# Linformer attention and a gated feed-forward in one kernel: an earlier V projection in the first batch, reciprocals spread over slots in the second, and a split last output tile

## The chip, the core and the metric

The kernel runs on one core of a Trainium2 chip. The metric is the device time of one execution in microseconds (us); lower is better. Seven executions of the kernel before took 569.02 to 571.19 us, with a median of 570.72 us. One more was recorded by the hardware profiler; its times are the ones that the text works with.

The engines are called as the profile calls them: PE is TensorE (matmuls; PEld are its weight loads), DVE is VectorE, ACT is ScalarE, POOL is GpSimd and SP is SyncE, which here only issues DMAs.

## The reference

Two stages follow each other. B = 8 batches, H = 8 heads, S = 1024 positions, head width 64, 64 projected keys, model width 512, feed-forward width 1536:

```python
k_proj = einsum('ks,bhsd->bhkd', E, k)
v_proj = einsum('ks,bhsd->bhkd', F, v)
scores = matmul(q, k_proj.T) / sqrt(64)
attn = exp(scores - max) / (sum(exp(scores - max)) + 1e-09)
x = (attn @ v_proj)          # heads side by side: 8192 tokens x 512
gate = sigmoid(x @ w_gate)
out = (gate * (x @ w_val)) @ w_out
```

The kernel computes in bf16 with fp32 sums. It leaves out the maximum, since the scores are small, and writes the sigmoid as (tanh(x/2) + 1)/2; the halves are taken up by a factor 0.5 when an output tile leaves PSUM.

## The kernel before, in words

**Work.** Each batch has two blocks of 512 tokens. For a block the feed-forward runs 12 steps (`mstep`, m = 0 to 11): 4 matmuls of 128x128 by 512 columns for the gate into one PSUM bank, 4 for the value into another, then `gate`: ACT takes the tanh of the gate's bank (L224, `sig`), and DVE multiplies it into the value's bank and writes `hT` (L930). Afterwards `oproj` multiplies `hT` with `w_out`: 12 matmuls for each of four tiles of 128 tokens, DVE moves the tile from PSUM to `ost` (L957), and SP writes it out (L965). The feed-forward uses four PSUM banks (F0 to F3) in turn: a bank that an `mstep` fills must have been emptied by the `mstep` two before.

**Attention** for the next batch lies between these steps. In the program the main loop makes a list `todo` of slots (an `mstep` or an `oproj` each), and `put(i, fn)` places a piece of attention behind slot i; `spots` lists those places. Every engine takes its instructions strictly in the order in which the program adds them, and a semaphore wait holds up all that is behind it on that engine. The pieces are: the projection of k and v (`project`), the turning of k (`turn_k`), scores and their exponentials (`sc`, ACT writes `eT`), the spread sums (`den`: matmuls that leave the sum of exponentials of each query in PSUM, then reciprocals on DVE into `rden`), `split` (DVE writes the reciprocal as two bf16 parts into `rhl`), `bc` (matmuls spread `rhl` over 64 partitions, ACT copies the result to `rb`) and `xo` (attention times V, DVE multiplies with `rb` and writes `xT`, the input of the feed-forward).

**The first batch** has no feed-forward to lie beside. Its first half is computed at the very start, in an order written out by hand (L975 to L1006): k projected in two halves of four heads (`project`, `keep_k`, `turn_k`), q turned on PE (`qt(0)`, `qt(1)`), `sc(0)`, `den(0)`, `sc(1)`, V's first half (`v_part(0)`), `den(1)`, `bc(0)`, `xo(0)`, `bc(1)`, V's second half (`v_part(1)`), and then `xo(1)`, which is called from inside the first feed-forward step (`first_pair`, L898), behind its first two matmuls. `first_pair` first multiplies with the input rows that `xo(0)` wrote and then with those of `xo(1)`. `busy(n)` puts n matmuls of the identity into an otherwise unused bank. The banks for this stage come from a list, `whole` (L202). All loads go through POOL in the order k, q, v, then the weights in chunks (`start_loads`); each is a DMA on one queue.

**The second batch's attention** (`attention(1)`) lies in the second block of the first batch: slot 11 is the steps m = 0 and 1 of that block (`first_pair`), slots 12 to 21 are m = 2 to 11, and 22 to 25 are the four `oproj` of the first block. Its `den` (L761 to L780) is one piece: eight matmuls, then four reciprocals of 128x128 (L776), then behind the same slot 18 `split` (L785, L787); `bc(0)` is behind slot 21.

**The end.** After the last step the four output tiles of the last block are done one behind the other (L1082); nothing else is left then. SP waits for the last four writes (L1085).

Of the kernel before, what the change touches and what calls it, by code (L numbers as in the profile page):

```python
# [7 lines left out]
ALU = mybir.AluOpType  # L8
# [4 lines left out]
P = 128  # L13
# [105 lines left out]
def bass_linformer_attn__then__ffn_glu_sigmoid_kernel(  # L119
# [18 lines left out]
    with contextlib.ExitStack() as es:  # L138
# [52 lines left out]
        class Ring:  # L191
# [8 lines left out]
        A0, A1, A2, A3 = AB  # L200
        F0, F1, F2, F3 = FB
        whole = Ring(  # L202
            (A0, A1, A2, A3, F0, F1)
            + (A0, A1, F2, A2)
            + (A3, F0, F1)
            + (A0, A1, A3, F0)
            + (A2, F2, A0, A1, F1)
            + (A2, A3, A0, A1, A2, A3)
        )
        ffn, att = Ring(FB), Ring(AB)  # L210

        def mm(b, o, lhsT, rhs, r, start=True, stop=True, tp=None, tr=False):
            kw = {}
            if tp is not None:
                kw["tile_position"] = tp
            if tr:
                kw["is_transpose"] = True
            else:
                kw["start"], kw["stop"] = start, stop
            return add("PE", lambda e: e.matmul(o, lhsT, rhs, **kw), r=r, x=[("bank", b)])  # L220
# [5 lines left out]
        def dve(fn, r, w, b=None):  # L226
            x = [] if b is None else [("bank", b)]
            return add("DVE", fn, r=r, w=w, x=x)
# [218 lines left out]
        def busy(n):  # L447
            for _ in range(n):
                mm(FB[3], bank[FB[3]][:, 0:P], ident[:, :], ident[:, :], ["ident"])
# [47 lines left out]
        def turn_k(ring, R=None):  # L497
            bk = ring.next()
            ob = bank[bk][:, :].bitcast(BF16)
            rs = range(NR)[pairs(R)]  # L500
            for n, r in enumerate(rs):
                for g in range(2):
                    mm(
                        bk,
                        ob[64 * g : 64 * g + 64, n * P : (n + 1) * P],
                        kp[:, r, :],
                        ident[:, :],
                        [("kp", r // 2), "ident"],
                        tr=True,
                        tp=(0, 64 * g),  # L510
                    )
            act(
                kpD[:, 2 * rs[0] : 2 * rs[-1] + 2, :].rearrange("p h c -> p (h c)"),
                ob[:, 0 : P * len(rs)],
                [],
                [("kpD", x) for x in both(R)],
                b=bk,
            )
# [152 lines left out]

        def attention(b):
            s = b % 2

            def kv():
                bk = att.next()
# [81 lines left out]
            def den():  # L758
                bk = att.next()
                for rnd in range(2):  # L760
                    for j in range(4):  # L761
                        n = 4 * rnd + j
                        mm(
                            bk,
                            bank[bk][32 * j : 32 * j + 32, :],
                            dsel[:, n % 2, rnd, :],
                            eT[:, n, :],
                            [("dsel", n % 2), ("eT", n)],
                            start=(rnd == 0),
                            stop=(rnd == 1),  # L770
                            tp=(0, 32 * j),
                        )
                for c in range(4):
                    cc = slice(c * P, (c + 1) * P)
                    dve(
                        lambda e, cc=cc: e.reciprocal(rden[:, cc], bank[bk][:, cc]),  # L776
                        [],
                        [("rden", c, R) for R in range(2)],
                        b=bk,
                    )  # L780

            def split():
                rd = [("rden", c, R) for c in range(4) for R in range(2)]
# [74 lines left out]
            if b == 1:  # L858
                return [
                    k_alone,  # L860
                    lambda: turn_k(att),
                    v_alone,
                    lambda: sc(0),
                    lambda: sc(1),
                    den,
                    split,
                    lambda: bc(0),
                    lambda: bc(1),
                    lambda: xo(0),
                    lambda: xo(1),  # L870
                ]
# [68 lines left out]
                b=pv,  # L940
            )

        def oproj(blk, tt, pb):
            T = 4 * blk + tt
            for m in range(NF):
                mm(
                    pb,
                    bank[pb][:, :],
                    hT[blk % 2][:, m, tt * P : (tt + 1) * P],
                    wO[:, m, :],  # L950
                    [("hT", blk % 2, m), "wO"],
                    start=(m == 0),
                    stop=(m == NF - 1),
                )
            o = ost[T % 4]
            dve(
                lambda e: e.tensor_scalar(o[:, :], bank[pb][:, :], 0.5, None, op0=ALU.mult),  # L957
                [],
                [("ost", T % 4)],
                b=pb,  # L960
            )
            t = 2 * (2 * (blk % 2) + tt % 2) + tt // 2
            add(
                "SP",
                lambda e: e.dma_start(out_v[blk // 2, t], o[:, :]),  # L965
                r=[("ost", T % 4)],
                dma=f"out{T % 4}",
            )


        start_loads()
# [1 line left out]
        project_consts()  # L973
        busy(6)
        qt, sc, den, bc, xo = half_unit(0, whole)  # L975
        for R in range(2):
            bk = whole.next()
            project(0, 0, [bk, bk], 0, R)
            busy(3)
            keep_k(bk, 0, R)  # L980
            turn_k(whole, R)
            if R == 0:
                busy(6)

        def v_part(R, engines):
            bks = [whole.next(), whole.next()]
            project(1, 1, bks, 0, R)
            keep_v(bks, 0, engines, R)

        qt(0, ("DVE", "ACT"))  # L990
        busy(3)
        sc(0)
        qt(1, ("DVE", "DVE"))
        busy(6)
        den(0)
        sc(1)
        busy(4)
        v_part(0, ["ACT"] * 4)
        den(1)
        bc(0)  # L1000
        busy(4)
        xo(0)
        busy(4)
        bc(1)
        busy(6)
        v_part(1, ["ACT", "DVE", "ACT", "DVE"])  # L1006
        load_q(1)
        load_k(1)
        load_v(1)
# [16 lines left out]
        for b in range(B):  # L1026
            todo = []
            for blk in (2 * b, 2 * b + 1):
                ms = [[m] for m in range(NF)]
                if blk <= 1:  # L1030
                    ms = [[0, 1]] + ms[2:]
                if blk == 1:
                    gaps = {11: [0, 1, 2, 3]}
                else:
                    gaps = {2: [0], 5: [1], 8: [2], 11: [3]}
                for m in ms:
                    if len(m) == 2:
                        todo.append(
                            lambda blk=blk: first_pair(blk, None if blk else lambda: xo(1))
                        )  # L1040
                    else:
                        todo.append(lambda blk=blk, m=m[0]: mstep(blk, m))
                    if blk >= 1:
                        for tt in gaps.get(m[-1], ()):
                            todo.append(lambda blk=blk, tt=tt: oproj(blk - 1, tt, ffn.next()))
            at = {}

            def put(i, fn):
                at.setdefault(i, []).append(fn)

            if b == 0:
                qt2, sc2, den2, bc2, xo2 = half_unit(1, att)
                put(4, lambda: (qt2(0, ("DVE", "ACT")), qt2(1, ("DVE", "ACT"))))
                put(5, lambda: (sc2(0), sc2(1)))
                put(6, den2)
                put(8, lambda: (bc2(0), bc2(1)))
                put(9, lambda: (xo2(0), xo2(1)))
                spots = (12, 13, 15, 16, 17, 18, 18, 21, 22, 23, 24)
            else:
                spots = (3, 6, 10, 13, 16, 16, 20, 23, 26, 29)  # L1060
            if b + 1 < B:
                for i, fn in zip(spots, attention(b + 1)):
                    put(i, fn)
            def load_next(n):
                load_k(n)
                load_q(n)
                load_v(n)

            if b == 0:
                put(16, lambda: load_next(2))  # L1070
                put(24, lambda: transpose_q(2))
            else:
                if b + 2 < B:
                    put(4, lambda b=b: load_next(b + 2))
                    put(20, lambda b=b: transpose_q(b + 2))
            for i, slot in enumerate(todo):
                slot()
                for fn in at.get(i, ()):
                    fn()
            assert max(at, default=0) < len(todo)  # L1080
        last = 2 * B - 1
        for tt in range(4):  # L1082
            oproj(last, tt, ffn.next())

        plan.emit(nc, es, final=[f"out{i}" for i in range(4)])  # L1085


# [26 lines left out]
```

The softmax here doesn't subtract the row's maximum and nothing guards it: scores larger than these inputs give would overflow.

## Time and profile before

| what | value |
|---|---|
| median of seven executions | 570.72 us (569.02 to 571.19) |
| the profiled execution's own time | 571.03 us |
| its span, first to last instruction | 569.2 us |
| PE busy | 551.6 us, 97% of the span |
| DVE, ACT, POOL busy | 249.3, 177.0, 107.2 us |
| feed-forward matmuls, gate / value / out | 747 / 752 / 750 records of 379 ns each, one every 0.2155 us where nothing waits |
| L776, the four reciprocals of 128x128 | 28 in seven batches, 909 ns each |
| L957, one output tile out of PSUM | 64, 692 ns each |

The time lies 1.83 us above the span; that part is outside of the program's instructions. A matmul record is longer than its share of the engine, since matmuls are pipelined: the distance from one start to the next is what counts. "Idle before <- releaser" in a row says how long the engine had nothing to do ahead of the instruction, and which engine's work (or DMA) let it go on. Idle time costs only where it lies on the chain that sets the end.

### The profile page before, as it was taken

What the parts mean: (1) busy time and instruction counts of PE and PEld (TensorE: products, weight loads), DVE (VectorE), ACT (ScalarE), POOL (GpSimd) and SP (SyncE); (2) the same over time, 40 slices, a digit from 0 to 9 for tenths busy, and PEclk for the clock granted to TensorE, in tenths of its full rate; (3) what the DMA queues carried; (4) which work ended last, traced back from release to release, by engine and by line L of the source; (5) the groups of instructions that cost most, each with busy time, mean ns of one, the idle gap of its engine ahead of it and who ended that gap; (6) DMA issues with size and microseconds to landing.
All of it is one profiled execution on the core that took longest, in us unless ns stands there. A gap on an engine that the chain in (4) does not pass through costs nothing.

```text
span 569.2 us, 7617 instructions
## 1 busy us (share of the span) xinstructions
PE 551.6 (97%) x2958; PEld 246.5 (43%) x3013; DVE 249.3 (44%) x398; ACT 177.0 (31%) x312; POOL 107.2 (19%) x148
## 2 busy tenths in 40 slices
PE   5999989999999999999999999999999999999997
PEld 4544434444444444444444444444444444444443
DVE  3644364344633546325443256335363354533332
ACT  2554631432133322352223422243213332222220
POOL 9400201007200090002600054000700007000000
PEclk9999999999999999999999999999999999999999
DMA  9999899935845059512677046560601001010012
GB/s 164 198 201 187 140 212 172 204 86 115 136 88 102 21 113 183 90 50 59 116 143 121 23 105 110 118 102 37 114 18 48 37 22 39 37 38 30 26 37 92
DMA packets 76420, 56.00 MB, mean 98 GB/s; under 512 B 34688, under 2 KB 67968, under 8 KB 76384
## 3 DMA queue, kind: packets, MB, share of 16 engines
q0 software_dynamic: 33984, 29.89, 34.7%
q1 hardware_dynamic: 42400, 25.63, 17.6%
q8 instruction: 23, 0.38, 0.3%
q14 instruction: 13, 0.11, 0.1%
HBM read 60.29 MB, written 16.78 MB: 135 GB/s over the span
## 4 chain that ended last, share of the span: by engine, by line
PE 94%; DVE 2%; DMA 1%; issue 1%; ACT 1%; POOL 0%; DVEq 0%; POOLq 0%
PE pF L220 87%; PE pA L220 7%; DMA KV<-in_k_dram 1%; ACT eT L224 1%; DVE rden L776 1%; DVE hT L930 0%; DVE xT L645 0%; ACT sig L224 0%; DVE rden L593 0%; DVE ost L957 0%; DVE vpD L495 0%; DVE rhi L785 0%; POOL quad L313 0%; DVE rhl L596 0%; DVE rhi L594 0%
## 5 line engine op out<-in xcount | busy, mean ns | idle before, releaser
L930 DVE SCALAR_TENSOR_TENSOR hT<-sig,pF 128x512 bf16<-128x512 f32 x192 | 130.7, 685 | 201.0 <-PE pF L220 146.8
L224 ACT ACTIVATE sig<-pF 128x512 f32<-128x512 f32 x192 | 114.4, 599 | 319.0 <-PE pF L220 315.4
L220 PE MATMUL pF<-xT,wV 128*128 128x512 bf16 x752 | 195.9, 379 | 2.7 <-DVE hT L930 1.9
L220 PE MATMUL pF<-xT,wG 128*128 128x512 bf16 x747 | 194.5, 379 | 2.5 <-issue 1.5
L220 PE MATMUL pF<-wO,hT 128*128 128x512 bf16 x750 | 173.9, 379 | 1.5 <-issue 0.8
L220 PEld LDWEIGHTS pF<-xT,wV 128*128 128x128 bf16 x768 | 74.9, 98 | 93.0 <-DVE hT L930 2.9
L220 PEld LDWEIGHTS pF<-wO,hT 128*128 128x128 bf16 x768 | 73.9, 98 | 93.0 <-issue 6.2
L220 PEld LDWEIGHTS pF<-xT,wG 128*128 128x128 bf16 x768 | 72.1, 98 | 95.0 <-issue 12.2
L822 POOL PARTITION_BROADCAST rb<-rrow x96 | 70.8, 798 | 217.1 <-DMA rrow<-rden 212.0
L957 DVE TENSOR_SCALAR ost<-pF 128x512 f32<-128x512 f32 x64 | 44.3, 692 | 103.7 <-PE pF L220 103.7
L224 ACT ACTIVATE eT<-pA 128x512 bf16<-128x512 f32 x63 | 32.7, 606 | 8.7 <-PE pA L220 8.7
L847 DVE TENSOR_TENSOR xT<-pA,rb 128x512 bf16<-128x512 f32 x56 | 34.7, 682 | 0.0
L776 DVE RECIPROCAL rden<-pA 128x128 f32<-128x128 f32 x28 | 23.7, 909 | 0.0
L238 POOL DMA_DIRECT2D KV<-in_v_dram x9 | 7.8, 874 | 84.4 <-PE pF L220 84.4
L220 PE MATMUL pA<-KV,EFT 128*64 128x512 bf16 (+2 forms) x168 | 16.0, 332 | 0.6 <-DMA KV<-in_k_dram 0.6
L224 ACT ACTIVATE kpd<-pA 64x1024 bf16<-64x1024 f32 x6 | 6.1, 1017 | 28.3 <-PE pA L220 28.3
L238 POOL DMA_DIRECT2D KV<-in_k_dram x9 | 8.0, 889 | 32.1 <-PE pF L220 32.1
L220 PEld LDWEIGHTS pA<-KV,EFT 128*64 128x64 bf16 x168 | 8.3, 115 | 8.1 <-issue 3.4
L220 PE MATMUL pA<-eT,vpD 64*64 64x512 bf16 (+1 forms) x140 | 10.4, 366 | 0.3 <-DVE vpD L495 0.3
L220 PE MATMUL pA<-qT,kpD 64*64 64x512 bf16 (+1 forms) x140 | 10.7, 370 | 0.0
L224 ACT ACTIVATE vpD<-pA 64x512 bf16<-64x512 f32 (+2 forms) x20 | 9.7, 485 | 1.6 <-PE pA L220 1.2
L238 POOL DMA_DIRECT2D Qb<-in_q_dram x11 | 9.4, 865 | 0.0
(70 smaller groups left out, 91.4 us busy)
## 6 DMA issues: line engine op xcount, KB each, us to landing
out_dram<-ost SPq DMA_DIRECT2D x64, 256.0 KB, 2.1
Qb<-in_q_dram POOLq DMA_DIRECT2D x7, 1024.0 KB, 15.3
KV<-in_k_dram POOLq DMA_DIRECT2D x7, 1024.0 KB, 11.2
KV<-in_v_dram POOLq DMA_DIRECT2D x7, 1024.0 KB, 11.7
wO<-in_moe_w_out_dram POOLq DMA_DIRECT2D x1, 1536.0 KB, 12.0
wG<-in_moe_w_gate_dram POOLq DMA_DIRECT2D x5, 256.0 KB, 18.4
wV<-in_moe_w_val_dram POOLq DMA_DIRECT2D x5, 256.0 KB, 19.0
KV<-in_k_dram POOLq DMA_DIRECT2D x2, 512.0 KB, 8.9
```

Source lines behind the costliest of these rows:

```text
L220: return add("PE", lambda e: e.matmul(o, lhsT, rhs, **kw), r=r, x=[("bank", b)])
L224: return add("ACT", lambda e: e.activation(o, i, func, scale=scale), r=r, w=w, x=x)
L238: add("POOL", lambda e: e.dma_start(o, i), r=r, w=w, dma=sem)
L776: lambda e, cc=cc: e.reciprocal(rden[:, cc], bank[bk][:, cc]),
L822: lambda e, n=n, i=2 * rnd + c, j=j, parts=parts: e.partition_broadcast(rb[0:parts, n, :], rrow[32 * j : 32 * j + 1, i, :], channels=parts),
L847: lambda e, r=r, g=g, n=n, bk=bks[g]: e.tensor_tensor(xT[s][:, r, :, 256 * g : 256 * g + 256], bank[bk][:, :].rearrange("p (f c) -> p f c" ...
L930: lambda e: e.scalar_tensor_tensor(hT[blk % 2][:, m, :], sg[:, :], 1.0, bank[pv][:, :], ALU.add, ALU.mult,),
L957: lambda e: e.tensor_scalar(o[:, :], bank[pb][:, :], 0.5, None, op0=ALU.mult),
```

## The change

There are three edits. The first is in the first batch: `qt(0)` comes ahead of the second `turn_k`, with three identity matmuls fewer; `v_part(1)` comes ahead of `bc(1)`, and its four copies out of PSUM are all on ACT (two were on DVE); four more identity matmuls go, and the list of banks is changed to fit. The second is in the second batch: V is projected behind slot 14 (it was 15), `sc` behind 15 and 16 (16 and 17), `den` behind 17 (18), the four reciprocals behind slots 17, 18, 19 and 20, and `split` behind 20 (18); `bc` and `xo` stay. The third is the last output tile: 12 matmuls of 384 columns and 12 of 128 into two banks, two copies out of PSUM, and two writes, the second with a semaphore of its own.

```diff
-            (A0, A1, A2, A3, F0, F1)
-            + (A0, A1, F2, A2)
+            (A0, A1, A2, A3, F0)
+            + (A0, A1, F1, F2, A2)
...
-            + (A2, A3, A0, A1, A2, A3)
+            + (A3, A2, A0, A1, A3, A2)
...
-                for c in range(4):
-                    cc = slice(c * P, (c + 1) * P)
-                    dve(
...
+                if b == 1:
+                    den_bank.append(bk)
+                else:
+                    for c in range(4):
+                        rec(c, bk)
+
+            def rec(c, bk):
+                cc = slice(c * P, (c + 1) * P)
+                dve(
+                    lambda e: e.reciprocal(rden[:, cc], bank[bk][:, cc]),
...
-                    den,
+                    lambda: (den(), rec(0, den_bank[0])),
+                    lambda: rec(1, den_bank[0]),
+                    lambda: rec(2, den_bank[0]),
+                    lambda: rec(3, den_bank[0]),
                     split,
...
-        def oproj(blk, tt, pb):
+        def oproj(blk, tt, pb, cols=((0, DM),)):
...
+            for n, (c0, c1) in enumerate(cols):
+                if n:
+                    pb = ffn.next()
...
+        k_part(0)
+        busy(3)
+        turn_k(whole, 0)
+        busy(6)
+        k_part(1)
+        busy(3)
         qt(0, ("DVE", "ACT"))
-        busy(3)
+        turn_k(whole, 1)
         sc(0)
...
         xo(0)
-        busy(4)
+        busy(6)
+        v_part(1)
         bc(1)
-        busy(6)
-        v_part(1, ["ACT", "DVE", "ACT", "DVE"])
...
-                spots = (12, 13, 15, 16, 17, 18, 18, 21, 22, 23, 24)
+                spots = (12, 13, 14, 15, 16, 17, 18, 19, 20, 20, 21, 22, 23, 24)
...
-            oproj(last, tt, ffn.next())
+            oproj(last, tt, ffn.next(), ((0, DM),) if tt < 3 else ((0, 384), (384, DM)))
```

In the new list of banks `bc(1)` fills A0 and A1 (A2 and A3 before) and `v_part(1)` fills A3 and A2 (A0 and A1 before). A0 was last filled by `bc(0)` and A1 by `xo(0)`.

More of the change, by code (lines that the diff above doesn't have):

```diff
@@ L673, in attention @@
             s = b % 2
+            den_bank = []
             def kv():
@@ L772, in den @@
                         )
-                for c in range(4):
-                    cc = slice(c * P, (c + 1) * P)
-                    dve(
[L776 to L780, printed above, removed]
+                if b == 1:
[7 more added lines that the diff above has]
+                    lambda e: e.reciprocal(rden[:, cc], bank[bk][:, cc]),
+                    [],
+                    [("rden", c, R) for R in range(2)],
+                    b=bk,
+                )
             def split():
@@ L941, in gate @@
             )
-        def oproj(blk, tt, pb):
+        def oproj(blk, tt, pb, cols=((0, DM),)):
             T = 4 * blk + tt
[L945 to L953, printed above, removed]
-                )
[L955 to L968, printed above, removed]
+            o = ost[T % 4]
+            t = 2 * (2 * (blk % 2) + tt % 2) + tt // 2
+            for n, (c0, c1) in enumerate(cols):
+                if n:
+                    pb = ffn.next()
+                for m in range(NF):
+                    mm(
+                        pb,
+                        bank[pb][:, 0 : c1 - c0],
+                        hT[blk % 2][:, m, tt * P : (tt + 1) * P],
+                        wO[:, m, c0:c1],
+                        [("hT", blk % 2, m), "wO"],
+                        start=(m == 0),
+                        stop=(m == NF - 1),
+                    )
+                dve(
+                    lambda e, pb=pb, c0=c0, c1=c1: e.tensor_scalar(
+                        o[:, c0:c1], bank[pb][:, 0 : c1 - c0], 0.5, None, op0=ALU.mult
+                    ),
+                    [],
+                    [("ost", T % 4, n)],
+                    b=pb,
+                )
+                add(
+                    "SP",
+                    lambda e, c0=c0, c1=c1: e.dma_start(out_v[blk // 2, t][:, c0:c1], o[:, c0:c1]),
+                    r=[("ost", T % 4, n)],
+                    dma=f"out{T % 4}" if n == 0 else "outlast",
+                )
         start_loads()
@@ L975, in bass_linformer_attn__then__ffn_glu_sigmoid_kernel, with k_part, v_part @@
         qt, sc, den, bc, xo = half_unit(0, whole)
-        for R in range(2):
+        def k_part(R):
             bk = whole.next()
             project(0, 0, [bk, bk], 0, R)
-            busy(3)
             keep_k(bk, 0, R)
-            turn_k(whole, R)
-            if R == 0:
-                busy(6)
-        def v_part(R, engines):
+        def v_part(R):
             bks = [whole.next(), whole.next()]
             project(1, 1, bks, 0, R)
-            keep_v(bks, 0, engines, R)
+            keep_v(bks, 0, ["ACT"] * 4, R)
+        k_part(0)
[4 more added lines that the diff above has]
+        busy(3)
         qt(0, ("DVE", "ACT"))
-        busy(3)
+        turn_k(whole, 1)
         sc(0)
@@ L997, in bass_linformer_attn__then__ffn_glu_sigmoid_kernel @@
         busy(4)
-        v_part(0, ["ACT"] * 4)
+        v_part(0)
         den(1)
@@ L1002, in bass_linformer_attn__then__ffn_glu_sigmoid_kernel @@
         xo(0)
-        busy(4)
+        busy(6)
+        v_part(1)
         bc(1)
-        busy(6)
-        v_part(1, ["ACT", "DVE", "ACT", "DVE"])
         load_q(1)
@@ L1082, in bass_linformer_attn__then__ffn_glu_sigmoid_kernel @@
         for tt in range(4):
-            oproj(last, tt, ffn.next())
-        plan.emit(nc, es, final=[f"out{i}" for i in range(4)])
+            oproj(last, tt, ffn.next(), ((0, DM),) if tt < 3 else ((0, 384), (384, DM)))
+        plan.emit(nc, es, final=[f"out{i}" for i in range(4)] + ["outlast"])
 _INS = ['q', 'k', 'v', 'E', 'F', 'moe_w_gate', 'moe_w_val', 'moe_w_out']
```

## The prediction

> **What bounds the kernel now.** I read the page first: PE is busy for 97% of the span, and the chain of work that ended last is PE for 94%. From 100 us to 552 us none of the three edits touches anything. So the question is only which of PE's few gaps the change closes. The chain in order of time puts those in three places, and the timeline (start, length, engine, line, operation, tiles, count, then the idle time before it and its releaser) shows each.
>
> ```profile
> PE 551.6 (97%) x2958; PEld 246.5 (43%) x3013; DVE 249.3 (44%) x398; ACT 177.0 (31%) x312; POOL 107.2 (19%) x148
> ```
>
> Start, the first batch:
>
> ```profile
> 13.48 0.43 PE L220 MATMUL pF<-ident,kp 128*64 128x128 bf16 x4
> 13.84 1.03 PE L220 MATMUL pA<-ident,Qb 128*128 128x128 bf16 x8
> ...
> 15.93 0.40 PE L220 MATMUL pA<-ident,Qb 128*128 128x128 bf16 x4
> ...
> 21.32 0.40 PE L220 MATMUL pA<-rhl,bsel 32*128 32x128 bf16 x8 [0.32 <-DVE rhl L596]
> ...
> 22.09 0.64 PE L220 MATMUL pA<-KV,EFT 128*64 128x128 bf16 x16
> ...
> 22.89 0.62 DVE L495 CAST vpD<-pA 64x128 bf16<-64x128 f32 x2 [0.30 <-PE pA L220]
> ...
> 24.20 1.29 DVE L645 TENSOR_TENSOR xT<-pA,rb 128x512 bf16<-128x512 f32 x2 [0.69 <-PE pA L220]
> ...
> 25.63 0.59 PE L220 MATMUL pF<-xT,wG 128*128 128x512 bf16 x2 [0.17 <-DVE xT L645]
> ```
>
> Here `bc(1)`, V's second half, its copies, `xo(1)` and two DVE products lie one behind the other, and from 25.63 PE runs without a gap until 33.13. What comes earlier than 25.63 moves all that follows.
>
> Second batch, the reciprocals:
>
> ```profile
> 70.00 3.38 DVE L776 RECIPROCAL rden<-pA 128x128 f32<-128x128 f32 x4
> 73.42 0.43 DVE L785 CAST rhi<-rden 128x512 bf16<-128x512 f32 x1
> 73.88 0.75 DVE L787 SCALAR_TENSOR_TENSOR rhl<-rhi,rows,rden 128x512 bf16<-128x512 bf16 x1
> 74.55 1.28 DVE L930 SCALAR_TENSOR_TENSOR hT<-sig,pF 128x512 bf16<-128x512 f32 x2
> 75.29 1.04 PE L220 MATMUL pF<-xT,wV 128*128 128x512 bf16 x4 [1.55 <-DVE hT L930]
> 76.26 0.39 PE L220 MATMUL pA<-rhl,bsel 32*128 32x512 bf16 x4
> ```
>
> DVE spends 4.6 us on the sums ahead of `hT`; PE's value matmuls of slot 21 need the bank that this `hT` empties, and stand.
>
> End:
>
> ```profile
> 552.76 13.11 PE L220 MATMUL pF<-wO,hT 128*128 128x512 bf16 x59
> 565.98 0.69 DVE L957 TENSOR_SCALAR ost<-pF 128x512 f32<-128x512 f32 x1 [1.90 <-PE pF L220]
> ```
>
> **Part 1, the start.** All the sums below take a semaphore's way from ACT or DVE to PE as 0.05 us (`rhl` ends 21.27, PE starts 21.32), to DVE or ACT from PE as 0.04 to 0.1, and a change of PE's tile form as 0.17 (the rows' "issue" gaps at 13.84 and 14.67).
>
> (a) The second half of k stands on PE until 12.9, three identity matmuls follow. `qt(0)` could begin at about 13.2, but its q quarter lands 10.3 us after its issue at 2.98, that is 13.28. So `qt(0)` starts at 13.33 instead of 13.84. Its 8 matmuls take 1.03: the first four give DVE its copy at 13.98 to 14.40, the last four give ACT its copy of 0.60 at 14.40 to 15.00. `turn_k` (0.36 from its start to the next group) follows at 14.25, `sc(0)` at 14.61 (was 15.13); its second half needs ACT's copy and starts at 15.05 (was 15.56). ACT's 0.38 us for `kpD` now lies at 15.0 to 15.4 and is over before the scores' end at 15.47. Gain 0.51. The second q quarter landed at 14.6, ahead of its use at 15.4.
>
> (b) I carry 0.51 on: `den(0)`, `sc(1)`, V's first half (18.22 becomes 17.71; this half lands at 4.44 + 12.7 = 17.14), `den(1)`, and `rhl` at 21.27 becomes 20.76. `xo(0)` ends, and behind six identity matmuls V's second half is projected at 20.6 (it lands at 5.2 + 14.5 = 19.7) and done at 21.24. ACT's four copies, at 0.285 us from one to the next (19.06 to 20.20 for the same four of the first half), fill 21.3 to 22.45. `bc(1)` would go at 21.25, but its bank A1 is read by DVE's first product of `xo(0)`, 21.30 to 21.99 before, so 20.79 to 21.48 now: that is a new wait, and `bc(1)` ends at 21.9. Its copies to `rb` are queued behind V's on ACT: 22.4 to 23.0 and 22.9 to 23.5. PE goes on with two gate matmuls at 22.2, then `xo(1)` at 22.8. DVE's two products start at 23.25 and, held by `rb`, 23.85, and end at 24.54. PE's six other matmuls of the first rows end at 24.45, and the second rows start at 24.66. Before: 25.63. **Gain of part 1: 0.97 us.** Behind it I compared landings with uses: the weights of the second rows land at 22.45, chunk 1 at 23.8 and 25.1 for uses at 26.2 and 27.0, chunk 3 at 33.1 for 34.8. The cover is 1.2 us or more; only if it were gone would the gain be lost.
>
> Bounds: all of (a) lost leaves 0.46; all of both 0; a copy chain on ACT hidden as in the row of the first half gives 1.2. I take 0.97.
>
> The clock is the risk. PE's 128-column matmuls take 314 ns at 13.84 and 219 ns from 15.93; eight q transposes stand 0.10 us apart in the first and 0.06 in the second. The array is slow until about 15.6 us. The change takes three identity matmuls out of this stretch and moves eight transposes forward in it.
> [...]
>
> **Part 2, the reciprocals.** I go by the old times and leave out the shift of part 1. With V behind slot 14 (`v_alone` 61.02 becomes 59.29), everything from it to `den` is one slot of 1.73 us earlier: `den` 68.64 becomes 66.90. The distances inside are the same, so ACT's copies and exponentials collide as before. Slots 18 to 21 then have their value matmuls at 68.38, 70.10, 71.83 and 73.56, and none waits for a bank. PE would come to `bc(0)` at 74.53 (76.25 less the 1.72 by which slot 21 was late).
> But `bc(0)` needs `rhl`, and DVE works in order. An `hT` starts 1.13 us behind the start of its value matmuls (550.17 to 551.30): for slots 18, 19 and 20 at 69.51, 71.23, 72.96, 0.69 each. A reciprocal of 0.91 behind each fits into 1.73. Behind slot 20 stand `hT` to 73.65, the last reciprocal to 74.48, `rhi` at 74.52, `rhl` 74.98 to 75.73. `bc(0)` starts at 75.77. So **the wait moves from slot 21 to `bc(0)` and keeps 1.24 of its 1.72 us; gain 0.48.** Queued behind `bc(0)` on PE are the four `oproj`, which need nothing of it and are late with it. The `hT` of slot 21 runs at 75.7 to 76.4 (76.43 to 77.12 before) and is needed by nobody until the next block's outputs.
> Bounds: a full new wait gives 0, none 1.72; the row of the four reciprocals itself says 0.48.
> Loads that are now used earlier: batch 1's V lands at 19.47 + 36.6 = 56.1, used at 58.3; its first two turned q parts at 56.2 and 57.1, used at 61.1; `w_out` at 60.08 + 12.0 = 72.1, used at 75.1. SP's and POOL's queues keep their order.
>
> **Part 3, the end.** Before: PE ends 565.87, DVE copies until 566.67, SP issues at 566.70 for 0.33, and the write lands 2.05 later, 568.75; the windows of half a microsecond show the DMAs at work only from 567.50, at 0.93 and then 0.48 of them, 0.7 us in all.
>
> ```profile
> 567.50:568.00 0.50, 0.00 (x0) 0.00 (x0) 0.00 (x0) 0.00 (x0) 0.00 (x0) 1.00 0.93 348
> 568.00:568.50 0.50, 0.00 (x0) 0.00 (x0) 0.00 (x0) 0.00 (x0) 0.00 (x0) 1.00 0.48 176
> ```
>
> After: 12 matmuls of 384 columns at three quarters of 0.2155 and 12 of 128 at 0.056 (six identity matmuls in 0.50, less the last one's 0.219, over five) cost 0.03 more. The 384 columns are ready at 565.23; DVE takes them until 565.9 (0.56, between 0.69 for 512 and 0.29 for the 128x128 rows), SP issues them until 566.26. The last 128 columns: PE to 565.90, DVE 0.29 to 566.30, issue at 566.33, which is 0.37 earlier. No copy of 128 columns from PSUM to fp32 is in the trace; 0.29 is the mean of the two `vpD` casts on DVE and of the 128x128 comparison, and the ends are 0.16 (a DVE operation on one column) and 0.69. The write moves a quarter of the bytes: 0.19 us if bytes set it, 0.7 if its 128 rows do, behind the first write's bytes, which end at about 567.3. So it lands between 567.98 and 568.5, a gain of 0.25 to 0.77; a second wait of SP costs nothing that a row shows. **I take 0.6.**
> [...]
>
> **Sum** against the profiled execution: 0.97 + 0.48 + 0.6 = 2.05, so 571.03 becomes 568.98. The median of the seven is 0.31 lower, which gives 568.67: **568.7 us**. A difference of over 0.2% (1.14 us) is about what a measurement of this kernel can tell from no change; that boundary is 569.58 and 571.86.
>
> **Rivals.** *The start gives nothing*: the array warms one step later, or a landing that I read as covered is not. For it: 0.05 us between the q quarter's landing and its use. Against it: every other landing is at least 0.5 us ahead. It leaves parts 2 and 3, 1.08 less: 569.6. Chance 0.14.
> *No new wait at `bc(0)`*: 1.72 instead of 0.48, 567.4. For it: only that ACT or DVE rows run closer than I placed them; against it, DVE's order. Chance 0.04.
> *Slower: the array stays slow into the feed-forward.* Seven identity matmuls fewer, and PE stands for up to 0.6 us around `bc(1)`. A slow array costs 40% of its spell (0.10 against 0.06). It decides from 5.1 us of slowness on (2.05/0.4), and is slower by over 0.2% from 8 us on; ten, from 15.6 to 25.6, cost 4.0: 572.7. Against it: PE stood 1.55 us at 73.7 and ran on at 0.2155. Chance 0.04.
> The forecast with its own range (567.9 to 569.5 by the bounds above): 0.78.
>
> The range goes from the forecast's low end to above the first rival, and the seven runs lie up to 1.7 us below and 0.5 above their median, so a median may sit 0.6 off: 567.2 to 570.2. For the chances I spread each case by 0.75 us for that: faster 0.78 x 0.88 + 0.14 x 0.5 + 0.04 = 0.80; slower 0.04 and a little of the rest, 0.05; same 0.15.
>
> **What would show it.** Right: `sc(0)` at about 14.6, the second rows' first gate matmuls at 24.7; no wait of PE for `hT` in slot 21 but about 1.2 us for `rhl` at `bc(0)`; the second last write issued 0.37 us earlier relative to PE's end. Wrong: 128-column matmuls of 314 ns after 16 us, a DMA as releaser at 13 to 35 us, a wait of PE in slots 18 to 20, or a last write that takes its 2.05 us whole.

## The result, and the profile after

The changed kernel takes 569.21 us (median of 17 executions, 567.57 to 569.6) against 570.72 us (median of 41). The ratio is 0.9976 (95% interval 0.9968 to 0.9984), so it is 1.4 us faster (0.9 to 1.8). The forecast was 568.7 us, in a range from 567.2 to 570.2: the side is right, the time lies in the range, and the gain is smaller than forecast. The two profiled executions differ by 1.76 us (571.03 and 569.27), where the sum said 2.05.

Executions of one and the same kernel differ by up to 2.5 us, nearly all of it in the start, as the spans further down show; so parts of the kernel are compared as stretches inside a trace, and medians compare whole kernels.

The page's row of engines, after:

```profile
PE 550.8 (97%) x2963; PEld 246.7 (43%) x3018; DVE 249.3 (44%) x397; ACT 177.4 (31%) x314; POOL 107.2 (19%) x148
```

It tells nothing of the gain: 1.7 us are 0.3% of the span, and the sums of busy time hardly move. The timeline of the start says more (columns as in the prediction: start, length, engine, line, operation, tiles, count, then the idle time and its releaser):

```profile
13.53 1.06 PE L220 MATMUL pA<-ident,Qb 128*128 128x128 bf16 x8
14.52 0.42 PE L220 MATMUL pF<-ident,kp 128*64 128x128 bf16 x4
15.61 0.40 PE L220 MATMUL pA<-ident,Qb 128*128 128x128 bf16 x4
...
21.02 0.64 PE L220 MATMUL pA<-KV,EFT 128*64 128x128 bf16 x16 [0.21 <-DMA KV<-in_v_dram]
...
21.59 0.54 PE L220 MATMUL pA<-rhl,bsel 32*128 32x128 bf16 x8
21.78 1.16 ACT L224 ACTIVATE vpD<-pA 64x128 bf16<-64x128 f32 x4 [0.77 <-PE pA L220]
22.96 1.09 ACT L224 ACTIVATE rb<-pA 128x512 f32<-128x512 f32 x2
23.59 1.29 DVE L645 TENSOR_TENSOR xT<-pA,rb 128x512 bf16<-128x512 f32 x2 [1.31 <-ACT rb L224]
...
25.02 0.59 PE L220 MATMUL pF<-xT,wG 128*128 128x512 bf16 x2 [0.22 <-DVE xT L645]
```

The order is the one foretold: `qt(0)` ahead of `turn_k`, V's second half ahead of `bc(1)`, ACT's six copies in one row, DVE's products held by `rb`. But a DMA now stands as a releaser at 21.02, which the prediction had named as a sign that it is wrong: PE waits 0.21 us for the second half of V. The second rows start at 25.02 (25.63 before, 24.66 forecast).

The second batch in the same timeline:

```profile
71.25 0.95 DVE L783 RECIPROCAL rden<-pA 128x128 f32<-128x128 f32 x1
72.37 0.69 DVE L940 SCALAR_TENSOR_TENSOR hT<-sig,pF 128x512 bf16<-128x512 f32 x1 [0.17 <-PE pF L220]
72.97 1.03 PE L220 MATMUL pF<-xT,wV 128*128 128x512 bf16 x4
72.98 0.95 DVE L783 RECIPROCAL rden<-pA 128x128 f32<-128x128 f32 x1
...
73.96 0.43 DVE L792 CAST rhi<-rden 128x512 bf16<-128x512 f32 x1
74.42 0.75 DVE L794 SCALAR_TENSOR_TENSOR rhl<-rhi,rows,rden 128x512 bf16<-128x512 bf16 x1
...
75.23 0.40 PE L220 MATMUL pA<-rhl,bsel 32*128 32x512 bf16 x4 [1.24 <-DVE rhl L794]
```

The value matmuls of slot 21 (72.97) wait for nothing any more; `bc(0)` waits 1.24 us for `rhl`, to the hundredth what was forecast (the last digit is luck: the gain of this part came out at 0.42, not 0.48). And the end:

```profile
551.74 13.14 PE L220 MATMUL pF<-wO,hT 128*128 128x512 bf16 x71
...
564.32 0.56 DVE L971 TENSOR_SCALAR ost<-pF 128x384 f32<-128x384 f32 x1 [1.26 <-PE pF L220]
564.91 0.33 SPq L980 DMA_DIRECT2D out_dram<-ost  x1
564.92 0.29 DVE L971 TENSOR_SCALAR ost<-pF 128x128 f32<-128x128 f32 x1
565.28 0.43 SPq L980 DMA_DIRECT2D out_dram<-ost  x1
```

The view of the DMA issues (KB each, median us from issue to landing) has the two writes apart:

```profile
out_dram<-ost SPq DMA_DIRECT2D x1, 192.0 KB, 1.9
out_dram<-ost SPq DMA_DIRECT2D x1, 64.0 KB, 1.7
```

From the first of the last block's output matmuls to the last issue it was 13.94 us (552.76 to 566.70) and is 13.54: 0.40 earlier. From that issue to the end of the span it was 2.50 and is 2.22. In the windows of half a microsecond the DMAs now stop between 566.5 and 567 (0.10 of them at work, then 0.00), half a microsecond and more ahead of the span's end at 567.5.

Between these places the two kernels run alike, so the span falls apart into four stretches (spans are read to 0.1 us):

| stretch | before | after | gain |
|---|---|---|---|
| start to the second rows' first gate matmuls | 25.63 | 25.02 | 0.61 |
| from there to `bc(0)` of the second batch | 50.63 | 50.21 | 0.42 |
| from there to the last block's output matmuls | 476.50 | 476.51 | -0.01 |
| from there to the end of the span | 16.44 | 15.76 | 0.68 |

### The profile page after: what moved, and what is told of

It reads as the page before. It is cut to its first block, busy times and chain, and to the rows that moved or that the text cites. A ratio compares the mean times of both kernels' runs of the same rounds, so it can differ in the third digit from the quotient of the medians.

```text
span 567.5 us, 7629 instructions
## 1 busy us (share of the span) xinstructions
PE 550.8 (97%) x2963; PEld 246.7 (43%) x3018; DVE 249.3 (44%) x397; ACT 177.4 (31%) x314; POOL 107.2 (19%) x148
## 3 DMA queue, kind: packets, MB, share of 16 engines
q1 hardware_dynamic: 42544, 25.63, 18.4%
## 4 chain that ended last, share of the span: by engine, by line
PE 95%; DVE 2%; DMA 1%; issue 1%; POOL 0%; DVEq 0%; POOLq 0%
PE pF L220 88%; PE pA L220 7%; DMA KV<-in_k_dram 1%; DVE xT L645 1%; DVE hT L940 0%; DVE rden L593 0%; DVE rden L783 0%; DVE rhl L794 0%; DVE rhi L792 0%; POOL quad L313 0%; DVE ost L971 0%; DVE rhi L594 0%; DVEq L102 0%; DVE rhl L596 0%; POOLq L1116 0%
## 5 line engine op out<-in xcount | busy, mean ns | idle before, releaser
L220 PE MATMUL pF<-wO,hT 128*128 128x512 bf16 (+2 forms) x762 | 173.9, 376 | 1.5 <-issue 0.8
L971 DVE TENSOR_SCALAR ost<-pF 128x512 f32<-128x512 f32 (+1 forms) x65 | 44.4, 684 | 103.5 <-PE pF L220 103.5
```

The source lines that it names most:

```text
L971: lambda e, pb=pb, c0=c0, c1=c1: e.tensor_scalar(o[:, c0:c1], bank[pb][:, 0 : c1 - c0], 0.5, None, op0=ALU.mult),
```

## The experiments

Two accounts of the start stood against each other. One is the prediction's: the new order is shorter by itself, and each execution moves it with the landing of k. In the other the landing of V's second half has become the bound, so that a start in which all else goes fast gains nothing; where the expectations speak of a theory B for the start, it is this one. For the other two parts the question was whether their gain is a constant.

**Each part alone.** Three kernels are the one before with one part of the change.

```diff
# e1_start: the hand-written order and the lists of banks of the change, the rest as before
# e2_rec: only spots = (12, 13, 14, 15, 16, 17, 18, 19, 20, 20, 21, 22, 23, 24), with rec(0) to rec(3)
# e3_tail: only ((0, DM),) if tt < 3 else ((0, 384), (384, DM))
```

> Part 1 alone (first batch), the rest as before. Theory A (the chain through ACT's and DVE's copies sets the start): the second rows' first gate matmuls start 0.8 to 1.0 us ahead of the kernel before, measured from the landing of k's first half, and the time falls by that, to about 569.9 us against 570.7. Theory B (the landing of V's second half sets it): PE's projection of V's second half shows the DMA as its releaser, as it did at 21.02 us in the changed kernel, and the gain follows that landing: 0.3 to 0.6 us. Theory C (the array warms later): matmuls of 128 columns of 314 ns after 16 us, no gain.

> Part 2 alone (second batch: reciprocals one to a slot, V one slot earlier). Theory A (DVE's order moves the wait to the sums' spreading): PE does not wait for hT in slot 21 but 1.2 us for rhl at bc(0), and the time falls by 0.4 to 0.5 us, to about 570.25. Rival (the wait only moves): gain within 0.1 us. Other rival (the stall goes): 1.7 us.

> Part 3 alone (last tile in 384 and 128 columns). Theory A: the last write is issued 0.3 to 0.4 us earlier and lands in 1.7 instead of 2.05 us, so the time falls by 0.6 us, to about 570.1. Rival (a write costs its fixed time): only the earlier issue is left, 0.3 us.

Timed against before, e1 gives 0.9996 (0.9985 to 1.0007), e2 0.9996 (0.9982 to 1.0009), e3 0.9992 (0.9980 to 1.0004): none of the three parts can be told from no change by itself, and each interval is 1.2 us wide or more. The stretches can: e2 has 50.21 from the second rows to `bc(0)` with the wait of 1.24 us, e1 and e3 have 50.62; e3 has 15.75 for the end, e1 and e2 have 16.5. So parts 2 and 3 are worth 0.42 and 0.68 with or without the others. Part 1 is no constant. The timeline of e1, at k's second half, at V's second half and at the second rows:

```profile
11.06 0.64 PE L220 MATMUL pF<-KV,EFT 128*64 128x128 bf16 x16 [0.41 <-DMA KV<-in_k_dram]
...
19.55 0.64 PE L220 MATMUL pA<-KV,EFT 128*64 128x128 bf16 x16 [0.42 <-DMA KV<-in_v_dram]
...
23.55 0.59 PE L220 MATMUL pF<-xT,wG 128*128 128x512 bf16 x2 [0.22 <-DVE xT L645]
```

and of e2, whose start is that of before:

```profile
10.84 0.64 PE L220 MATMUL pF<-KV,EFT 128*64 128x128 bf16 x16 [0.45 <-DMA KV<-in_k_dram]
...
23.57 0.59 PE L220 MATMUL pF<-xT,wG 128*128 128x512 bf16 x2 [0.17 <-DVE xT L645]
```

The old order reaches the second rows at the same moment as the new one, and both are 2 us earlier than in the profiled execution of before. In both the 16 matmuls of k's second half took 0.64 us, where they took 1.06 in before:

```profile
12.02 1.06 PE L220 MATMUL pF<-KV,EFT 128*64 128x128 bf16 x16
```

In e1 and e2 the array was fast from about 9.4 us on, in before from 15.9. And in e1 PE stands 0.42 us for V.

**Half of part 1.** e5 moves only `qt(0)`, e6 moves only `v_part(1)` with its copies on ACT.

```diff
# e5_q, against before
+        busy(3)
         qt(0, ("DVE", "ACT"))
-        busy(3)
+        turn_k(whole, 1)
         sc(0)
# e6_v, against before
-        busy(4)
+        busy(6)
+        v_part(1)
         bc(1)
-        busy(6)
-        v_part(1, ["ACT", "DVE", "ACT", "DVE"])
```

> Only the first half of part 1: q is turned ahead of the second turn_k, three identity matmuls fewer; V stays behind bc(1). Theory A (a chain of copies from the start on): the 0.5 us of this step are kept and the time falls by 0.4 to 0.5 us. Theory B (V's second half sets the start once the array is fast or the chain short): the second rows cannot start earlier than 4.0 us behind that landing, and the order with V behind bc(1) needs 4.2 us or more, so the gain is 0.5 us where the array starts slow (matmuls of k's second half over 1.06 us) and 0.1 or less where it starts fast (0.64 us).

> Only the second half of part 1: V's second half ahead of bc(1), its four copies on ACT; q and k as before. Theory A: 0.4 to 0.5 us less than before. Theory B: second rows 4.0 to 4.1 us behind the landing of V's second half if PE shows that DMA as releaser, later if not; gain 0.2 to 0.5 us where the array starts slow, 0.1 to 0.3 where it starts fast.

Measured: 0.9991 (0.9982 to 1.0000) for each, about half a microsecond with an interval that just touches none. In their traces V had landed ahead of its use (19.58 for 20.89, 20.07 for 20.79), and the second rows came at 24.43 and 25.00, which is 15.2 and 15.3 us behind the landing of k's first half and 4.9 us behind that of V. Which half of part 1 gives more cannot be told from these.

The starts of those profiled executions that have the old or the new order whole, in one table (us; landings are read to 0.1 us; "k" is the landing of k's first half, "fast" the moment from which 128-column matmuls take 0.22 instead of 0.31 us, "V" the landing of V's second half, "rows" the second rows):

| kernel | order | k | fast | V | rows | rows - k | rows - V | PE waits for V |
|---|---|---|---|---|---|---|---|---|
| before | old | 9.44 | 15.9 | 19.70 | 25.63 | 16.2 | 5.9 | no |
| e12, below | old | 9.74 | 15.9 | 21.36 | 25.86 | 16.1 | 4.5 | no |
| e2 | old | 8.14 | 9.3 | 19.38 | 23.57 | 15.4 | 4.2 | no |
| e3 | old | 8.54 | 9.8 | 19.37 | 23.72 | 15.2 | 4.4 | no |
| after | new | 9.64 | 15.4 | 20.97 | 25.02 | 15.4 | 4.05 | yes |
| e9, below | new | 9.34 | 15.5 | 20.97 | 25.08 | 15.7 | 4.1 | yes |
| e1 | new | 8.44 | 9.5 | 19.47 | 23.55 | 15.1 | 4.1 | yes |
| e4, below | new | 8.84 | 12.5 | 19.98 | 24.08 | 15.2 | 4.1 | yes |
| e13, below | new | 8.04 | 11 | 19.17 | 23.25 | 15.2 | 4.1 | yes |
| e11, below | new | 7.94 | 11.7 | 20.57 | 25.52 | 17.6 | 4.95 | yes |

Two columns answer the question. In the new order PE waits for V in every row, and the second rows come 4.05 to 4.1 us behind its landing, whatever k and the array did (e11 is apart: there the granted clock falls to 0.50 on the way): in after 0.05 to the projection, 0.76 to ACT's first copy, ACT's six copies, DVE's products. And with a fast array the old order needs 15.2 to 15.4 behind k where the new one needs 15.1 to 15.2: the gain is 0 to 0.3. Only with a slow array does the old order take 16.1 to 16.2 against 15.4 to 15.7, and gain 0.4 to 0.8. The second account holds, with this condition, as far as these few executions show.

**V later still.** The second half of V is loaded behind the upper half of the first weight chunk instead of ahead of it, in the changed kernel (e11) and in the one before (e12).

```diff
-            for R in range(2):
-                load_kv_heads(1, v, R)
-            load_w(0, 0)
+            load_kv_heads(1, v, 0)
+            load_w(0, 0)
+            load_kv_heads(1, v, 1)
```

> The changed kernel with the first weight chunk's upper half loaded ahead of V's second half, so that V's second half lands about 1.3 us later. Theory B (that landing sets the start): PE waits for it, the second rows start 4.0 to 4.1 us behind it as in the changed kernel, and the time rises by 0.8 to 1.3 us. Theory A (the copies' chain sets it): the lag shrinks below 4.0 and the time rises by 0.4 us or less.

> The kernel before with the same late landing of V's second half. Theory B: the old order is bound by it too then, with second rows 4.2 to 4.4 us behind the landing; where the array starts fast the time rises by 1 us or more, where it starts slow by less, since the old order had up to 1.6 us of slack (5.95 us of lag in the kernel before). The changed order, with the same late V, is then 0.1 to 0.4 us ahead in this stage. Theory A: no change from the kernel before.

e12 is 1.0000 (0.9991 to 1.0010): the old order has room for it, as theory A said. In its profiled execution V landed at 21.36 and was used at 22.32, with no wait. e11 is 0.9974 (0.9964 to 0.9985), against 0.9976 for the changed kernel. So the delay cost nothing that can be measured, each ratio being uncertain by about half a microsecond, and what theory B expected, 0.8 to 1.3 us in e11 and an old order bound by V in e12, did not come: a miss in both. Yet the one trace of e11 shows the mechanism at full size:

```profile
20.62 0.64 PE L220 MATMUL pA<-KV,EFT 128*64 128x128 bf16 x16 [1.96 <-DMA KV<-in_v_dram]
...
23.99 1.06 PE L220 MATMUL pF<-xT,wG 128*128 128x512 bf16 x2
...
25.52 0.59 PE L220 MATMUL pF<-xT,wG 128*128 128x512 bf16 x2
```

PE stands 1.96 us for V, and the second rows come at 25.52, 17.6 us behind k and 4.95 behind V. In this execution k landed at 7.94, the earliest of all, so PE came to V early, and some of that wait is time that the early start had won. Not all of it: in e13, below, with V loaded in the old place, k landed at 8.04 and the second rows came at 23.25. That is 2.3 us earlier, 1.4 by V's landing and 0.9 by the shorter way from there. The windows of one microsecond of e11 (the stretch and its length, busy time and count of PE, PEld, DVE, ACT, POOL, then the granted clock, the DMAs' share and GB/s) show what followed:

```profile
21.00:22.00 1.00, 1.00 (x20) 0.43 (x14) 0.00 (x0) 0.58 (x3) 0.00 (x0) 0.96 1.46 196
22.00:23.00 1.00, 0.60 (x9) 0.19 (x8) 0.00 (x0) 0.95 (x3) 0.00 (x0) 0.50 1.45 196
23.00:24.00 1.00, 1.00 (x11) 0.29 (x4) 0.64 (x2) 0.65 (x2) 0.00 (x0) 0.50 1.45 197
24.00:25.00 1.00, 1.00 (x4) 0.44 (x3) 0.65 (x2) 0.00 (x0) 0.00 (x0) 0.50 1.46 196
25.00:26.00 1.00, 1.00 (x6) 0.38 (x4) 0.00 (x0) 0.00 (x0) 0.00 (x0) 0.83 1.45 196
```

The granted clock falls to 0.50 from about 22 to 25.3 us. Four of e11's nine executions, this one among them, list a mean granted clock of 0.997, which is what 3.4 us at half the clock make of a span of 568 us; the other five list 1.000, and no execution of the changed kernel lists less than 0.999. That is what the prediction's slower rival speaks of, an array that is slow into the feed-forward, here behind a longer wait than the changed kernel has. That the wait brought it on is not shown.

How often the executions without a profile are bound by V stays open, but their starts can be worked out from their spans. From the second rows to the end of the span it is 543.6 us in all five profiled executions with the second batch and the end of before (before, e1, e5, e6, e12), 542.5 in after and e11, and 541.2 in e4 and e8, below; so a span less that is a start. The middle start is 25.3 us in before (30 executions, timed beside e1), 24.9 in the changed kernel and 25.0 in e1: part 1 is worth 0.3 to 0.4 us in the middle execution.

**The wait that part 2 left.** e4 takes the changed kernel and lets the sums start one reciprocal earlier: two reciprocals behind slot 17, the third behind 18, the last and `split` behind 19.

```diff
-                spots = (12, 13, 14, 15, 16, 17, 18, 19, 20, 20, 21, 22, 23, 24)
+                spots = (12, 13, 14, 15, 16, 17, 17, 18, 19, 19, 21, 22, 23, 24)
```

> The changed kernel with other slots for the reciprocals: two behind slot 17, one behind 18, the last and the split behind 19. Theory A (PE waits at bc(0) only because DVE idles 0.2 to 0.3 us in each slot and puts the last reciprocal and the split behind a late hT): rhl is ready at about 73.7 us on the changed kernel's clock, PE comes to bc(0) at 74.0 and does not wait; no value matmul waits for a bank, since hT of slot 18 ends at 70.1 and its bank is needed at 71.2. Time 1.2 us below the changed kernel, about 568.0. Rival (DVE has no room): a value matmul of slot 20 or 21 waits for hT, and 0.5 us or more of it comes back: 568.5 to 569.2.

Measured: 567.05 us (566.39 to 568.35), ratio to before 0.9947 (0.9929 to 0.9966), that is 3.0 us faster than before, where the changed kernel is 1.4 us faster. It beats both. The timeline shows why:

```profile
66.72 1.76 DVE L783 RECIPROCAL rden<-pA 128x128 f32<-128x128 f32 x2
68.40 0.63 DVE L940 SCALAR_TENSOR_TENSOR hT<-sig,pF 128x512 bf16<-128x512 f32 x1
68.94 0.94 DVE L783 RECIPROCAL rden<-pA 128x128 f32<-128x128 f32 x1
70.35 0.94 DVE L783 RECIPROCAL rden<-pA 128x128 f32<-128x128 f32 x1
71.33 0.43 DVE L792 CAST rhi<-rden 128x512 bf16<-128x512 f32 x1
71.79 0.75 DVE L794 SCALAR_TENSOR_TENSOR rhl<-rhi,rows,rden 128x512 bf16<-128x512 bf16 x1
...
72.98 0.39 PE L220 MATMUL pA<-rhl,bsel 32*128 32x512 bf16 x4
```

`rhl` ends at 72.54, and `bc(0)` starts at 72.98 without a wait. From the second rows to `bc(0)` it takes 48.90 instead of 50.21: 1.31 us, the whole of the wait that was left. No value matmul waits for a bank, since the two `hT` that are late (72.46) are late by less than their banks' slack. Against the changed kernel the medians say 2.2 us and the ratios 1.65. What is above 1.31 lies in the starts: by the spans the middle start of e4's seven executions is 24.0, 0.9 us ahead of the changed kernel's 24.9, although this stage is the same in both.

**V's copies shared again.** e8 is e4 with the second half's copies on ACT and DVE in turn, to shorten ACT's row of six.

```diff
-            keep_v(bks, 0, ["ACT"] * 4, R)
+            keep_v(bks, 0, ["ACT", "DVE", "ACT", "DVE"] if R else ["ACT"] * 4, R)
```

> The changed kernel with two reciprocals behind slot 17 (as in the run before) and, in the first batch, V's second half copied by ACT and DVE in turn instead of ACT alone. Theory B (the second rows wait for V's landing, its projection, four copies, two copies of the spread sums and a product, 4.0 us): two copies of 0.29 us leave ACT, DVE has just ended its products of xo(0) and does them in 0.6, so the way from the landing to the second rows falls from 4.0 to 3.7 or 3.8 us and the time by 0.2 to 0.3 us below the run before, to about 566.8 us. Rival (DVE's products are late by what it takes over): no gain, 567.05.

Measured: 567.79 us, 0.9948 (0.9932 to 0.9964), the same as e4; the rival is right. The timeline:

```profile
18.61 1.01 POOL L238 DMA_DIRECT2D KV<-in_k_dram  x1
18.85 0.82 DVE L594 CAST rhi<-rden 64x128 bf16<-64x128 f32 x1
19.47 1.02 POOL L238 DMA_DIRECT2D KV<-in_v_dram  x1
...
20.70 0.68 DVE L645 TENSOR_TENSOR xT<-pF,rb 128x512 bf16<-128x512 f32 x1
21.41 0.62 DVE L495 CAST vpD<-pA 64x128 bf16<-64x128 f32 x2
...
22.18 0.41 PE L220 MATMUL pA<-eT,vpD 64*64 64x256 bf16 x8
```

DVE comes to its two casts only at 21.41, behind its products of `xo(0)`, and `xo(1)` starts at 22.18, 2.5 us behind V's landing (19.67), where e4 needs 2.1 (22.07 and 19.98). But in this execution the cast `rhi`, which lies ahead of these products, took 0.82 us (0.59 in e4, 0.22 at its shortest). Whether shared copies would gain where that cast is short is not shown.

**Other splits of the last tile.**

```diff
-((0, 384), (384, DM))
+((0, 256), (256, DM))    # e9_half
+((0, 448), (448, DM))    # e13_448
```

> The changed kernel with its last tile in 256 and 256 columns. From the start of the last matmuls to the end of the span the kernel before took 16.44 us, the changed one 15.76. Theory A (the last write's bytes count beside its issue): DVE's last copy of 256 columns takes 0.15 us more than that of 128 and the write moves twice the bytes, so 0.3 us are given back: 16.05. Rival (the write's fixed time is all): only DVE's 0.15, 15.9.

> The changed kernel with its last tile in 448 and 64 columns. From the start of the last matmuls to the end of the span: 15.76 us with 384 and 128. If only DVE's last copy counts, 64 columns are 0.07 us shorter and it is 15.7, unless SP is still issuing the first write when the second is ready. [...]

The end takes 15.91 us in e9 and 16.24 in e13, against 15.76 with 384 columns and 16.44 with one write; for e9 that is the rival's 15.9. Each is one execution with its span read to 0.1 us, so the issues below weigh more than the 0.15 us between e9 and the changed kernel. The end of e9 and then that of e13:

```profile
564.98 0.42 DVE L971 TENSOR_SCALAR ost<-pF 128x256 f32<-128x256 f32 x1 [0.81 <-PE pF L220]
565.43 0.33 SPq L980 DMA_DIRECT2D out_dram<-ost  x1
```

```profile
562.87 0.63 DVE L971 TENSOR_SCALAR ost<-pF 128x448 f32<-128x448 f32 x1 [1.58 <-PE pF L220]
563.41 0.21 DVE L971 TENSOR_SCALAR ost<-pF 128x64 f32<-128x64 f32 x1
563.52 0.33 SPq L980 DMA_DIRECT2D out_dram<-ost  x1
563.90 0.43 SPq L980 DMA_DIRECT2D out_dram<-ost  x1
```

With halves the last copy is longer (0.42 instead of 0.29), and the issue lies 13.64 us behind the output matmuls' start (13.54 with 384 and 128). With 64 columns the copy is shorter, but it is done at 563.62, while SP is at the first issue until 563.85: the second comes at 563.90, 13.94 behind the start, as late as in the kernel before. What is left of the gain is the landing, 1.8 us instead of 2.05. Of the three splits 384 and 128 columns is the best: the first part must be copied and issued before the last one is ready.

## Why the prediction was right, and where its numbers were off

**Part 1** was 0.97 and measured 0.61. Its order of events was right: PE's start of `qt(0)` was forecast at 13.33 and came at 13.53, and k's landing was 0.20 later in this execution (9.64 against 9.44). The step that failed is "every other landing is at least 0.5 us ahead", with V read as landing at 19.7 for a use at 20.6. That number was right for the one execution that it was read from; in the profiled execution of after V landed at 20.97, and over the executions it lies between 19.2 and 21.0. Part of that is a shift that k has too. What counts against the cover is how far V lands behind k, since PE's work follows k: 10.3 us in before, 11.3 in after, and 10.3 to 11.6 over the profiled executions with V in its place, which is more than the cover of 0.9. What sets this distance is not shown. The projection came at 21.02: 0.20 by k, 0.21 by the wait for V. From there to the second rows it took 4.00, where the working had 4.06 (20.6 to 24.66). 0.20 and 0.21 less 0.06 are the 0.36 that the second rows lie behind the forecast (25.02 against 24.66), up to rounding. Measured from k's landing part 1 gave 0.81 in this pair. That both profiled executions had an array slow until 15.4 us or later is luck: with the starts of e2 and e1 the gain would have read 0.02 (23.57 and 23.55). Over many executions part 1 is worth less: the 1.4 us of the ratio less 0.42 and 0.68 leave 0.3, and the middle starts say 0.3 to 0.4. The first rival ("the start gives nothing") thus comes close (0 to 0.3 us) for the profiled executions whose array is fast early, by the mechanism that it named second, a landing read as covered. The prediction took its base from one start and asked only whether the change could make the array later; it didn't ask what the change is worth when the array is fast early in both kernels.

**Part 2** was 0.48 and measured 0.42. The wait moved from slot 21 to `bc(0)` and kept 1.24 us, as worked out from DVE's order; e4 removes just this wait and gains 1.31. That the sum is 0.06 short is within what I read the rows to. The rival without a wait fell.

**Part 3** was 0.6 and measured 0.68. The issue is 0.40 earlier (0.37 forecast), DVE's copies take 0.56 and 0.29 (0.56 and 0.29 forecast), and the smaller write gives 0.28 us from its issue to the end (0.23 taken). PE's tail is 13.14 against 13.11, the 0.03 forecast.
The price list that was missing can now be read off the runs: from issue to landing 2.05 us for 256 KB, 1.9 for 192, 1.8 for 128, 1.7 for 64 and 1.8 for 32 KB, read to 0.1 us. A quarter of the bytes saves 0.35 us and an eighth 0.25; the bytes are a small part of a write's time. In before the DMAs moved data for 0.7 of the last write's 2.05 us, which leaves 1.35 us without; the fastest of these writes took 1.7 us in all.

**The slower rival** did not come in the changed kernel, where PE stood 0.21 us for V and 0.51 us behind `bc(1)` (22.64), and 128-column matmuls were fast from 15.4 us on. e11 shows that such a spell does come.

What stays open: how the executions without a profile divide between starts bound by V and others; what each half of part 1 gives; and whether 256-byte rows have a price of their own in the 32 KB write of e13, since only 0.1 us over the 64 KB write speaks for it.

## What to carry to other kernels

When work at the start of a kernel is pulled forward, compare each landing with its use in more than one execution: a cover of 0.9 us is none when one load lands up to 1.3 us earlier or later behind another, and the gain ends where the first load is waited for. When a stall is removed, look at the engine that caused it: as long as DVE did the same work in the same place, the wait only moved (0.42 of 1.72 us gained), and starting that work one slot earlier gave the other 1.31. For a last write, split so that the first part's copy and issue are over when the last part is ready; here 128 of 512 columns did that, and both 256 and 64 were worse (one execution each).

## What the runs showed of the hardware

The moment at which the array becomes fast differs by 7 us (9.0 in e8, 15.9 in e12), though k's first half landed only 1.1 us apart in the two (8.64 and 9.74). The profile's granted clock reads 1.00 during the slow stretch at the start too (in before in every microsecond from 9 to 16): only the matmuls' durations tell (1.06 or 0.64 us for the same 16).

In e11 a wait of 1.96 us, with PE busy for 0.66, 0.00 and 0.38 of the three microseconds from 18 to 21, was followed by 3.4 us at a granted clock of 0.50, which began 1.3 us after PE's matmuls had set in again. In before a stall of 1.55 us was not: PE was busy for all of each microsecond from 70 to 73 and again from 75.3 to 76.3, and the granted clock stayed at 1.00. What brings such a spell on is not shown.

DVE's cast of 64x128 from SBUF to SBUF (`rhi`) takes 0.22 us when POOL is quiet (in before at 20.66, POOL's last issue having ended at 20.51) and up to 0.82 us next to POOL's DMA issues (after 0.47, e4 0.59, e11 0.66, e8 0.82). Being next to an issue is not enough. Of the 26 such casts in the thirteen traces, fifteen took 0.26 us or more; each of these began 0.24 us or more behind the start of an issue and ended 0.04 or 0.05 us behind its end, as e8's does in the rows above (18.85 to 19.67, the issue from 18.61 to 19.62). The other eleven took 0.22 or 0.23 us, among them ones that began within 0.20 us of an issue's start (e12 at 18.87, in the issue from 18.67 to 19.68). In the changed kernel it lies on the way to `rhl`, but V's landing was later still. No run here takes POOL's issues away, so what makes the cast long is not shown.
